# A delta-rule recurrence feeding a cosine-gated network: block inverses in halves for the first two pairs, and the cosine's argument in radians

## The chip, the cores and the metric

The kernel runs on one core of a Trainium2 chip. The metric is the device time of one execution in microseconds; the time before is 710.78 us, the median of three runs (709.21 to 710.8). The profile shown below is of one execution of 709.21 us; from its first to its last instruction it spans 707.4 us, and all times of the profile count from its start.

The engines have these names: PE is TensorE (matmul; PEld its weight loads), DVE is VectorE, ACT is ScalarE, POOL is GpSimd, SP is SyncE, which here only issues DMA transfers. All five run side by side and wait for one another by semaphores. Each takes its own instructions in order.

## The reference

Two stages. The first is a delta rule for 4 × 8 heads, 768 steps, head dimension 48; the second is a network with the gate h · cos(h).

```python
# q, k, v: (4, 8, 768, 48), beta: (4, 8, 768); all float32
k_n = k / (norm(k, axis=-1) + 1e-6)
state = zeros((B, H, D, D))
for t in range(S):
    y[:, :, t] = einsum('bhd,bhde->bhe', q[:, :, t], state)
    v_old = einsum('bhde,bhd->bhe', state, k_n[:, :, t])
    state = state + bt[..., None, None] * einsum('bhd,bhe->bhde', k_n[:, :, t], v[:, :, t] - v_old)

x = y.transpose(0, 2, 1, 3).reshape(3072, 384)
h = x @ w_in            # 384 x 2048
g = h * cos(h)
out = g @ w_out         # 2048 x 384
```

## The kernel before

**Units and pairs.** The 768 steps are cut into 24 units of C = 32 steps; two units make a pair, so there are 12 pairs. Within a unit the 32 steps depend on each other through a strictly lower triangular 32 × 32 matrix L per head (the products of keys, scaled by beta): the new values u solve (1 + L) u = r, with r the values less what the state holds for the keys. The kernel computes Z = (1 + L)⁻¹, which needs no state and so can be made ahead, and applies it by matmuls when the state arrives.

**The inverse.** For a pair, the matrices of 2 units × 8 heads × 4 batches stand one per partition (64, each twice: the two halves of the partitions take every other row of Z). The tile gb comes there through DRAM, since the rearrangement goes across partitions. The elimination takes one column j at a time, two operations each. Pair 0 is done on VectorE with Z in PSUM, all others on GpSimd with Z in SBUF. Z then goes through DRAM again (z_dr) and comes back as zt, arranged for TensorE.

```python
def invert(m, tag, columns):
    a, z = gbs[m], zs[m]
    eng = nc.gpsimd if tag is None else nc.vector
    for j in columns:                       # 31 of them
        rows = j // SPLIT + 1
        shape = [128, rows, C - 1 - j]
        ...
        eng.tensor_tensor(out=part, in0=z[:, 0:rows, j, None].to_broadcast(shape),
                          in1=a[:, j, None, j + 1 :].to_broadcast(shape), op=ALU.mult)
        behind = z[:, 0:rows, j + 1 :]
        eng.tensor_tensor(out=behind, in0=behind, in1=part, op=ALU.subtract)
```

**A unit's way through the recurrence.** turn (transposes of k and q) and gram (products of keys, and of keys and queries) prepare a unit. Then come, in a chain from unit to unit:

```python
through_state(n)   # PE:  p_kq <- st, kq_t          keys and queries times the state
right_side(n)      # DVE: rhs = vp - p_kq           (unit 0: rhs is vp)
solve(n)           # PE:  p_u <- zt, rhs            32 small matmuls
solve_out(n)       # DVE: u = p_u * bz
update(n)          # PE:  p_s <- kp, u
update_out(n)      # DVE: st = st + p_s
within(n)          # PE:  p_kq += tt, u
within_out(n)      # ACT: y <- p_kq
features(n)        # PE:  p_z <- transposes of y
features_out(n)    # ACT: x_ffn <- p_z              half of the pair's 256 tokens
```

p_u and p_z use the same PSUM bank ("one"), of which there is a single buffer.

**The network.** For a pair (256 tokens), eight blocks of two hidden tiles pass through:

```python
def hidden(p, f):          # PE: p_h <- x_ffn, w_in; 6 float32 matmuls, 12 records in the trace; two PSUM buffers
TURN = 1.0 / (2.0 * math.pi * SCALE)

def hidden_turns(p, f):    # ACT: whole turns, as int32
    nc.scalar.activation(turns[p, f], p_hs[p, f], AF.Copy, scale=TURN)

def hidden_rest(p, f):     # DVE, one operation: the rest, in turns
    nc.vector.scalar_tensor_tensor(out=r, in0=p_hs[p, f], scalar=TURN, in1=turns.pop((p, f)),
                                   op0=ALU.mult, op1=ALU.subtract)

def hidden_cos(p, f):      # ACT, two operations
    nc.scalar.activation(r, r, AF.Abs)
    nc.scalar.activation(r, r, AF.Sin, bias=halfpi, scale=-2.0 * math.pi)

def hidden_gate(p, f):     # DVE: g_ffn = r * p_h; frees the buffer of p_h
```

The products with w_out follow: plain for pair 0, and for all other pairs by Strassen's scheme (7 products for 8, with sums of parts of g_ffn and of w_out made on VectorE). The weights arrive as float64 words and are narrowed in the kernel: 12 tiles of w_in and 16 of w_out, each with two operations on ScalarE, two on VectorE and one on GpSimd.

**The order.** The kernel adds each of these steps as a task with an engine, an assumed cost, what it depends on, which buffers it takes and by when it is due. A list scheduler in Python (`Order`) then lays the tasks out in the order in which they are emitted and pins each engine's instructions to that order. So a change of assumed costs or dues moves instructions everywhere. [...] A few of its settings:

```python
WINDOW = 133.06; STICK = 4.14
W_IN, W_OUT, LOADS = 62.2, 48.42, -16.83
START = 64.59; FIRST, STEP = 4.18, 5.64      # dues of the blocks of the network
```

Of the kernel before, what the change touches and what calls it, by code (L numbers as in the profile page):

```python
# [11 lines left out]
FP = mybir.dt.float32  # L12
# [5 lines left out]
C = 32  # L18
DP = 64
SPLIT = 2  # L20


SCALE = 256.0


def _consts():

    p = np.arange(128)
    share = p // 64
    row = SPLIT * np.arange(C // SPLIT)[None, :] + share[:, None]
    return np.concatenate(
        [
            np.eye(128),
            p[:, None] % C < np.arange(C)[None, :],
            p[:, None] // C % 2 == np.arange(2)[None, :],  # L40
            (row[:, :, None] == np.arange(C)).reshape(128, -1),
        ],
        axis=1,
    ).astype(np.float32)


class Order:
# [8 lines left out]

    WINDOW = 133.06
    LAG = {"PE": 0.2, "DVE": 0.15, "ACT": 0.15, "POOL": 0.2, "SP": 2.0}
    IN_FLIGHT = 8
    STICK = 4.14  # L60
    CHANGE = 0.15
    SMALL = ("gram", "state", "solve", "update", "within")


    BLOCK, PHASE, AHEAD, FETCH = 256, 63, 38, 3.5
    COUNT = {
        "turn": 16, "gram": 128, "state": 256, "solve": 128, "update": 64, "within": 128,
        "features": 6, "hidden": 24, "out": 16,
# [151 lines left out]
def kernel(  # L220
# [43 lines left out]
    ROWS = C // SPLIT  # L264
    GBS, ZS = 2, 2
    GATES = 9
    LEAD = 3
# [65 lines left out]
    consts = const.tile(list(consts_np.shape), FP, name="consts")  # L333
    near = 130 + C
    for cols in (slice(0, near), slice(near, consts_np.shape[1])):
# [3 lines left out]
    odd = consts[:, 128 + C : 130 + C]  # L339
    eye = consts[:, 130 + C :].rearrange("p (r i) -> p r i", i=C)  # L340

# [173 lines left out]
    def gram_keys(n):  # L515
        g = gs[n] = work.tile([128, H, C], FP, name="g")
        bs = scales[n // 2][0][:, n % 2]
        nc.vector.tensor_tensor(
            out=by_parity(g),
            in0=p_gs[n][:, :, :, 0],  # L520
            in1=bs.rearrange("p (j a) -> p a j", a=2)[:, :, :, None].to_broadcast(wide),
            op=ALU.mult,
        )
# [10 lines left out]
    def gram_put(n):  # L534
        m = n // 2
        if m not in gbs:
            gbs[m] = dram.tile([2, H, B, C, C], FP, name="g_dr")
        nc.sync.dma_start(
            out=gbs[m][n % 2].rearrange("h b j i -> (b j) h i"), in_=gs.pop(n)
        )  # L540
# [11 lines left out]
    def invert_eye(m, tag):  # L552
# [4 lines left out]
        nc.scalar.copy(zs[m], eye)  # L557

    def invert(m, tag, columns):

        a, z = gbs[m], zs[m]
        eng = nc.gpsimd if tag is None else nc.vector
        for j in columns:
            rows = j // SPLIT + 1
            shape = [128, rows, C - 1 - j]
            if tag is None:
                part = work.tile([128, ROWS * C // 2], FP, name="part")  # L570
            else:
                part = ffn_pool.tile([128, ROWS * C // 2], FP, name="part_v", tag="o")
            part = part[:, 0 : shape[1] * shape[2]].rearrange(
                "p (r i) -> p r i", i=shape[2]
            )
            eng.tensor_tensor(  # L576
                out=part,
                in0=z[:, 0:rows, j, None].to_broadcast(shape),
                in1=a[:, j, None, j + 1 :].to_broadcast(shape),
                op=ALU.mult,  # L580
            )
            behind = z[:, 0:rows, j + 1 :]
            eng.tensor_tensor(out=behind, in0=behind, in1=part, op=ALU.subtract)  # L583
# [55 lines left out]

    def solve(n):  # L640
        zt, rhs = zts.pop(n), rhss.pop(n)
        p_u = p_us[n] = bank("one", [128, H, D], "p_u")
        for h in range(H):
            for b in range(B):
                nc.tensor.matmul(  # L645
                    p_u[quarter(b), h], zt[quarter(b), h], rhs[quarter(b), h]
                )

    def solve_out(n):

        u = us[n] = work.tile([128, H, 2, D], FP, name="u")
        wide = [128, H, 2, D]
        nc.vector.tensor_tensor(  # L653
            out=u,
            in0=p_us.pop(n)[:, :, None, :].to_broadcast(wide),
            in1=scales[n // 2][1][:, n % 2, :, :, None].to_broadcast(wide),
            op=ALU.mult,
        )
# [68 lines left out]

    TURN = 1.0 / (2.0 * math.pi * SCALE)

    def hidden_turns(p, f):  # L730
        turns[p, f] = ffn_pool.tile([128, 2, TOK], I32, name="turns")
        nc.scalar.activation(turns[p, f], p_hs[p, f], AF.Copy, scale=TURN)  # L732

    def hidden_rest(p, f):
        r = rests[p, f] = ffn_pool.tile([128, 2, TOK], FP, name="r")
        nc.vector.scalar_tensor_tensor(  # L736
            out=r, in0=p_hs[p, f], scalar=TURN, in1=turns.pop((p, f)),
            op0=ALU.mult, op1=ALU.subtract,
        )

    def hidden_cos(p, f):
        r = rests[p, f]
        nc.scalar.activation(r, r, AF.Abs)  # L743
        nc.scalar.activation(r, r, AF.Sin, bias=halfpi, scale=-2.0 * math.pi)  # L744

# [116 lines left out]
    def store(p, i):  # L862
# [9 lines left out]
            two=1, kq=1, one=1, h=2, vp=2, ksum=2, scales=4, kq_t=LEAD + 1,  # L872
            tt=LEAD + 1, g_gram=2, g_dr=3, gb=GBS, z=ZS, z_dr=3, zt=2, rhs=2, u=2, y=2,
            x=2, turns=2, r=2, g=GATES, o=2, o_out=2,
# [4 lines left out]
    VECTOR = {0: "one"}  # L879
    W_IN, W_OUT, LOADS = 62.2, 48.42, -16.83  # L880
    PLAIN = range(1)
    outs_done = [None]
    START = 64.59
    FIRST, STEP = 4.18, 5.64
    BASE = [START + (8 * FIRST + (p - 1) * 8 * STEP if p else 0) for p in range(NU // 2 + 2)]

    def inverse(m):
# [8 lines left out]
        deps = [("eye", m), ("gram_get", m)]  # L896
        ends = [0, 4, 8, 12, 16, 20, 24, C - 1]
        for i, (x, y) in enumerate(zip(ends, ends[1:])):
            each = (0.2, 0.001) if held else (0.323, 0.00178)
            cost = sum(  # L900
                2 * (each[0] + each[1] * (j // SPLIT + 1) * (C - 1 - j)) for j in range(x, y)
            )
            add(("inv", m, i), "DVE" if held else "POOL", cost,
                lambda x=x, y=y: invert(m, held, range(x, y)), deps,
                uses=[("gb", m)] if y == C - 1 else [])
            deps = [("inv", m, i)]
# [7 lines left out]
    def unit(n):  # L914
# [55 lines left out]
        if second:  # L970
# [9 lines left out]
            uses=[("vp", m)] if n else [])  # L980
        add(("solve", n), "PE", 0.75, lambda: solve(n), [("right", n), ("get", n)],
            makes=[("one", ("p_u", n))], uses=[("zt", n), ("rhs", n) if n else ("vp", m)])
        add(("solve_out", n), "DVE", 1.0, lambda: solve_out(n), [("solve", n), scaled],
# [17 lines left out]
    def gated(p):  # L1001
        for f in range(0, FT, 2):
# [3 lines left out]
            if p or f:  # L1006
# [6 lines left out]
                [("hidden", *key)], makes=[("turns", ("turns", *key))])  # L1013
            add(("rest", *key), "DVE", 0.73, lambda f=f: hidden_rest(p, f),
                [("turns", *key)], makes=[("r", ("r", *key))], uses=[("turns", *key)])
# [170 lines left out]
```

## Time and profile before

| what | value |
|---|---|
| time, median of 3 | 710.78 us |
| span of the profile | 707.4 us |
| PE busy | 642.0 us, 91% |
| DVE busy | 400.3 us, 57% |
| POOL busy | 344.1 us, 49% |
| ACT busy | 281.5 us, 40% |
| granted TensorE clock, mean | 0.955 |

The page of a profile gives, for each engine, its busy time, then the span in 40 equal slices with the busy share of each in tenths (9 is 90% or more), and the granted clock of TensorE in tenths of full speed. A group of instructions is named by its line in the kernel, its engine and "output<-inputs"; x is how often it ran, and the idle time of its engine ahead of it is given with what ended it. A busy TensorE is not one at its peak: the ends of matmuls are modelled. In the timeline a row is: start in us, duration in us, engine, line, operation, and in brackets the idle time ahead of it with what ended that.

### The profile page before, as it was taken

What the parts mean: (1) busy time and instruction counts of PE and PEld (TensorE: products, weight loads), DVE (VectorE), ACT (ScalarE), POOL (GpSimd) and SP (SyncE); (2) the same over time, 40 slices, a digit from 0 to 9 for tenths busy, and PEclk for the clock granted to TensorE, in tenths of its full rate; (3) what the DMA queues carried; (4) which work ended last, traced back from release to release, by engine and by line L of the source; (5) the groups of instructions that cost most, each with busy time, mean ns of one, the idle gap of its engine ahead of it and who ended that gap; (6) DMA issues with size and microseconds to landing.
All of it is one profiled execution on the core that took longest, in us unless ns stands there. A gap on an engine that the chain in (4) does not pass through costs nothing.

```text
span 707.4 us, 25090 instructions
## 1 busy us (share of the span) xinstructions
PE 642.0 (91%) x11000; PEld 564.3 (80%) x11000; DVE 400.3 (57%) x804; ACT 281.5 (40%) x482; POOL 344.1 (49%) x738
## 2 busy tenths in 40 slices
PE   3206989999999999999999999999999999999985
PEld 2205767768988988988988988988989989988975
DVE  4995568967655645546546546545635535544441
ACT  4423467742443532532533533533433433432420
POOL 6468957868608508518518518518318328200000
PEclk9555899999999999999999999999999999999999
DMA  9888663562223233133223133231221220100000
GB/s 176 211 161 197 122 193 80 135 125 58 36 56 71 39 64 67 32 74 66 45 60 66 29 77 64 38 74 37 38 51 37 37 52 14 31 23 4 1 23 22
DMA packets 162700, 49.25 MB, mean 70 GB/s; under 512 B 154208, under 2 KB 157296, under 8 KB 162592
## 3 DMA queue, kind: packets, MB, share of 16 engines
q1 hardware_dynamic: 161120, 46.82, 32.1%
q8 instruction: 86, 1.41, 0.9%
q0 software_dynamic: 384, 0.64, 0.4%
q10 hardware_dynamic: 1088, 0.20, 0.2%
q14 instruction: 22, 0.18, 0.1%
HBM read 36.62 MB, written 11.01 MB: 67 GB/s over the span
## 4 chain that ended last, share of the span: by engine, by line
PE 85%; DMA 4%; POOL 3%; DVE 3%; issue 2%; ACT 1%; SPq 1%; ACTq 0%; DVEq 0%; POOLq 0%
PE p_h L719 35%; PE p_out L805 30%; PE p_kq L618 4%; PE p_kq L683 3%; PE p_s L666 3%; PE p_out L761 3%; PE p_u L645 3%; PE p_t L489 2%; PE p_g L507 2%; DMA pairs<-in_moe_w_in_dram 2%; POOL part L576 1%; POOL z L583 1%; DMA qp<-in_q_dram 1%; DMA gb<-g_dr 1%; DMA kp<-in_k_dram 1%
## 5 line engine op out<-in xcount | busy, mean ns | idle before, releaser
L719 PE MATMUL p_h<-x_ffn,w_in 128*128 128x256 f32 x1152 | 264.9, 383 | 2.4 <-DVE g_ffn L751 1.6
L719 PEld LDWEIGHTS p_h<-x_ffn,w_in 128*128 128x128 f32 x1152 | 216.9, 191 | 32.0 <-DVE g_ffn L751 1.5
L576 POOL TENSOR_TENSOR part<-z,gb 128x126 f32<-128x126 f32 (+22 forms) x341 | 136.1, 399 | 210.7 <-DMA gb<-g_dr 185.3
L583 POOL TENSOR_TENSOR z<-z,part 128x126 f32<-128x126 f32 (+22 forms) x341 | 134.3, 394 | 26.7
L805 PE MATMUL p_out<-w_out,g_ffn 128*128 128x192 f32 x704 | 133.6, 334 | 2.8 <-DVE o L853 1.6
L736 DVE SCALAR_TENSOR_TENSOR r<-p_h,turns 128x512 f32<-128x512 f32 x96 | 66.1, 689 | 113.8 <-ACT turns L732 113.7
L732 ACT ACTIVATE turns<-p_h 128x512 int32<-128x512 f32 x96 | 56.9, 592 | 169.1 <-PE p_h L719 169.0
L805 PEld LDWEIGHTS p_out<-w_out,g_ffn 128*128 128x128 f32 x704 | 113.6, 190 | 9.5 <-ACT o L842 3.3
L805 PE MATMUL p_out<-w_sum,g_ffn 128*128 128x192 f32 x528 | 96.3, 329 | 1.8 <-DVE o L853 1.8
L751 DVE TENSOR_TENSOR g_ffn<-r,p_h 128x512 f32<-128x512 f32 x96 | 65.6, 683 | 48.0 <-ACT r L744 48.0
L805 PEld LDWEIGHTS p_out<-w_sum,g_ffn 128*128 128x128 f32 x528 | 86.3, 190 | 4.9 <-DVE o L853 3.1
L821 DVE TENSOR_TENSOR g_ffn<-g_ffn 128x256 f32<-128x256 f32 x176 | 80.5, 480 | 10.8 <-PE p_out L805 8.9
L743 ACT ACTIVATE r<-r 128x512 f32<-128x512 f32 x96 | 60.7, 632 | 58.2 <-DVE r L736 58.1
L744 ACT ACTIVATE r<-r,halfpi 128x512 f32<-128x512 f32 x96 | 69.3, 722 | 3.1
L853 DVE SCALAR_TENSOR_TENSOR o<-p_out,o 128x192 f32<-128x192 f32 x77 | 26.5, 356 | 59.7 <-PE p_out L805 59.2
L489 PE MATMUL p_t<-consts,kp 128*128 128x128 f32 x96 | 16.9, 306 | 41.9 <-DMA vp<-in_v_dram 29.5
L489 PEld LDWEIGHTS p_t<-consts,kp 128*128 128x128 f32 x96 | 12.9, 157 | 44.6 <-issue 38.5
L694 ACT COPY y<-p_kq 128x384 f32<-128x384 f32 x24 | 11.5, 478 | 76.7 <-PE p_kq L683 76.7
L448 POOL TENSOR_TENSOR knrm<-ksum,halves 128x16 f32<-128x16 f32 (+1 forms) x14 | 36.4, 2602 | 9.8 <-DVE ksum L436 7.6
L618 PEld LDWEIGHTS p_kq<-st,kq_t 48*32 48x32 f32 x2944 | 29.5, 106 | 9.6 <-issue 8.8
L618 PE MATMUL p_kq<-st,kq_t 48*32 48x48 f32 x2944 | 33.1, 215 | 3.9 <-issue 3.2
L653 DVE TENSOR_TENSOR u<-p_u,bz 128x768 f32<-128x768 f32 x24 | 23.0, 956 | 17.1 <-PE p_u L645 17.1
(65 smaller groups left out, 547.0 us busy)
## 6 DMA issues: line engine op xcount, KB each, us to landing
pairs<-in_moe_w_in_dram SPq DMA_DIRECT2D x12, 512.0 KB
gb<-g_dr SPq DMA_DIRECT2D x24, 256.0 KB
pairs<-in_moe_w_out_dram SPq DMA_DIRECT2D x16, 384.0 KB
vp<-in_v_dram SPq DMA_DIRECT2D x96, 48.0 KB
out_dram<-o SPq DMA_DIRECT2D x24, 192.0 KB
kp<-in_k_dram SPq DMA_DIRECT2D x92, 48.0 KB
qp<-in_q_dram SPq DMA_DIRECT2D x92, 48.0 KB
g_dr<-g SPq DMA_DIRECT2D x24, 128.0 KB
```

Source lines behind the costliest of these rows:

```text
L489: nc.tensor.transpose(p_t[:, a, j], src[:, 2 * j : 2 * j + 2], ident)
L576: eng.tensor_tensor(out=part, in0=z[:, 0:rows, j, None].to_broadcast(shape), in1=a[:, j, None, j + 1 :].to_broadcast(shape), op=ALU.mult,)
L583: eng.tensor_tensor(out=behind, in0=behind, in1=part, op=ALU.subtract)
L618: nc.tensor.matmul(p_kq[quarter(b), par, a, j], kq_t[rows48(par), a, j, quarter(b)], st[rows48(par), b // 2, j, b % 2], start=(j == 0 and ...
L719: nc.tensor.matmul(p_h[:, i], w_in[:, t, (f + i) * 128 : (f + i + 1) * 128], xts[p][:, t], start=(t == 0), stop=(t == KT - 1),)
L732: nc.scalar.activation(turns[p, f], p_hs[p, f], AF.Copy, scale=TURN)
L736: nc.vector.scalar_tensor_tensor(out=r, in0=p_hs[p, f], scalar=TURN, in1=turns.pop((p, f)), op0=ALU.mult, op1=ALU.subtract,)
L743: nc.scalar.activation(r, r, AF.Abs)
L744: nc.scalar.activation(r, r, AF.Sin, bias=halfpi, scale=-2.0 * math.pi)
L751: nc.vector.tensor_tensor(out=gates[p, f // 4][:, f % 4 : f % 4 + 2], in0=rests.pop((p, f)), in1=p_hs.pop((p, f)), op=ALU.mult,)
L805: nc.tensor.matmul(p_o, left(p, e // 2, a)[:, e % 2], right(e, b), start=(e == 0), stop=(e == FT // 2 - 1), skip_group_check=True,)
L821: nc.vector.tensor_tensor(out=left(p, k, to), in0=left(p, k, one), in1=left(p, k, two), op=op)
```

## The change

It has two parts, which replace one another in the sense that the kernel after has the first and not the second.

**Halves.** For pairs 0 and 1 only the two diagonal 16 × 16 blocks of 1 + L are inverted, both in the same operations (one more dimension of two). Z is then the inverse of the block diagonal part alone, and what lies below it is handled in the solve, with vectors: v = Z r gives the first 16 rows of u; a cross product with L of the first half, subtracted from the second half of r; and a second product with Z. For this the tile g of a unit is kept in SBUF until its cross product. The aim is a shorter inverse at the start, where everything waits for the first one. The tile u has one buffer instead of two.

**Radians.** The cosine's argument is no longer kept in turns. The rest is h less 2π times the whole turns, and 2π stands in two parts for accuracy, so hidden_rest has two VectorE operations per block where it had one. The scheduler's cost for it is set to 1.45 instead of 0.73, and its settings are other ones.

```diff
-    WINDOW = 133.06
-    STICK = 4.14
+    WINDOW = 82.51
+    STICK = 2.55
...
+    HALVED = range(2)
+    GRAMS = 4
...
     def invert(m, tag, columns):
...
+        n = C // 2 if m in HALVED else C
         for j in columns:
             rows = j // SPLIT + 1
-            shape = [128, rows, C - 1 - j]
+            shape = [128, rows, n - 1 - j]
+            if n < C:
+                shape = [128, 2] + shape[1:]
...
+                column = twice(column, (ROWS // 2) * C + n)
+                row = twice(row, n * C + n)
+                behind = twice(behind, (ROWS // 2) * C + n)
...
+    def solve_half(n):
+        p_us[n] = bank("one", [128, H, D], "p_u")
+        quarters(p_us[n], zts[n], rhss[n])
+
+    def half_out(n):
+        v = us[n] = work.tile([128, H, D], FP, name="y")
+        nc.scalar.activation(v, p_us.pop(n), AF.Copy, scale=first_half)
+
+    def cross(n):
+        p_us[n] = bank("one", [128, H, D], "p_u")
+        quarters(p_us[n], gs.pop(n), us.pop(n))
+
+    def cross_out(n):
+        rhs = work.tile([128, H, D], FP, name="rhs")
+        nc.vector.scalar_tensor_tensor(
+            out=rhs, in0=p_us.pop(n), scalar=less_second, in1=rhss[n],
+            op0=ALU.mult, op1=ALU.add,
+        )
+        rhss[n] = rhs
...
     def hidden_rest(p, f):
         r = rests[p, f] = ffn_pool.tile([128, 2, TOK], FP, name="r")
+        n = turns.pop((p, f))
         nc.vector.scalar_tensor_tensor(
-            out=r, in0=p_hs[p, f], scalar=TURN, in1=turns.pop((p, f)),
-            op0=ALU.mult, op1=ALU.subtract,
+            out=r, in0=n, scalar=-PI2_HI * SCALE, in1=p_hs[p, f], op0=ALU.mult, op1=ALU.add
+        )
+        nc.vector.scalar_tensor_tensor(
+            out=r, in0=n, scalar=-PI2_LO * SCALE, in1=r, op0=ALU.mult, op1=ALU.add
         )
...
-    W_IN, W_OUT, LOADS = 62.2, 48.42, -16.83
+    W_IN, W_OUT, LOADS = 57.87, 99.73, 3.15
-    START = 64.59
-    FIRST, STEP = 4.18, 5.64
+    START = 35.79
+    FIRST, STEP = 3.55, 5.99
...
+        if m in HALVED:
+            ends = [0, 4, 8, C // 2 - 1]
...
-            add(("rest", *key), "DVE", 0.73, lambda f=f: hidden_rest(p, f),
+            add(("rest", *key), "DVE", 1.45, lambda f=f: hidden_rest(p, f),
                 [("turns", *key)], makes=[("r", ("r", *key))], uses=[("turns", *key)])
```

In the order of the changed kernel, the first blocks of p_h again stand right behind the chain of unit 1, and each of units 0 to 3 has its half-solve, cross product and solve in a row, with other work of TensorE between some of them.

## The prediction

> **What bounds the kernel now.** I read the page's slices first, then the busy time by stage, then the timeline of the first 80 us, then the waits of TensorE after it. The slices (40 of 17.7 us; digits are tenths):
>
> ```profile
> PE   3206989999999999999999999999999999999985
> DVE  4995568967655645546546546545635535544441
> PEclk9555899999999999999999999999999999999999
> DMA  9888663562223233133223133231221220100000
> ```
>
> TensorE is full from about the fifth slice to the end. Before that it is mostly idle at half clock while the DMA engines are full. The first matmul of the network (p_h, L719) stands at 79.15 us, so I cut the span there, at 160 and at 675:
>
> ```profile
> 0.00:79.15 79.15, 30.60 (x950) 25.81 (x951) 54.59 (x147) 29.48 (x53) 52.68 (x90) 0.63 0.86 178
> 79.15:160.00 80.85, 76.13 (x1109) 59.13 (x1103) 59.47 (x108) 49.42 (x91) 61.36 (x95) 0.98 0.56 132
> 160.00:675.00 515.00, 512.46 (x8823) 458.90 (x8822) 277.39 (x526) 200.29 (x335) 230.11 (x556) 1.00 0.24 46
> ```
>
> (Columns: busy us and count of PE, PEld, DVE, ACT, POOL; clock; DMA share; GB/s.) In the long middle TensorE idles 2.5 of 515 us: nothing but less TensorE work can shorten it. In the second stretch it idles 4.7 us. Only the head has room: 48.5 idle us. The two longest waits of TensorE after the head hardly count:
>
> ```profile
> PE p_h L719 <- issue: 0.8, 2, 0.6
> PE p_out L805 <- DVE o L853: 0.4, 2, 0.2
> ```
>
> So the span is the time of the first p_h plus a nearly fixed 628 us of TensorE work. What fixes 79.15 is in the timeline:
>
> ```profile
> 27.63 0.19 DVE L576 TENSOR_TENSOR part_v<-p_i,gb 128x31 f32<-128x31 f32 x1 [0.50 <-DMA gb<-g_dr]
> 45.57 0.18 DVE L583 TENSOR_TENSOR p_i<-p_i,part_v 128x16 f32<-128x16 f32 x1
> 46.79 0.69 SPq L592 DMA_DIRECT2D z_dr<-z  x1
> 52.42 4.53 SPq L601 DMA_DIRECT2D zt<-z_dr  x8
> 57.04 2.01 PE L645 MATMUL p_u<-vp,zt 32*32 32x48 f32 x64 [1.65 <-issue]
> 79.15 5.45 PE L719 MATMUL p_h<-x_ffn,w_in 128*128 128x256 f32 x24
> ```
>
> The first inverse runs on VectorE from 27.63 to 45.75. It is stored to DRAM at 46.79 and fetched back by eight issues from 52.42 to 56.95. The first solve starts at 57.04, and the recurrence through units 0 and 1 takes 22.1 us more. SyncE issues almost without a pause from 0.75 to 70 us (a load of four DMAs takes it 1.9 to 4.3 us). That queue is as much a limit of the head as the inverse is.
>
> **What the Trainium skill says.** "VectorE: DVE Perf Modes", section on the errata: an fp32 operation with two tensors takes (N+151)/0.96 ns, so 691 ns for 512 elements. The trace agrees: 689 ns for r<-p_h,turns. The same page, section "Why `tensor_tensor` can't do 2×_2P or 4×", says the second tensor occupies the second read port. So I give the new second operation no faster mode, although it reads SBUF only; the SBUF-only L410 of this shape has a median of 686 ns. "TensorE: Matmul & The Clock Gate", Part 1: the clock is halved until TensorE has been busy for a few microseconds. The trace agrees: clock 0.63 in the head, and a solve of 64 matmul records takes 1.55 to 2.01 us there and 0.88 us at 88.5 us. "DMA: Bandwidth & Descriptors", section on small descriptors, says short ones cost more per byte; 154,208 of the 162,700 packets here are under 512 B, in agreement with DMA at 0.86 and only 178 GB/s in the head.
>
> **The change, part by part.**
>
> *Inverse of pair 0.* It had 31 columns of two operations and has now 15, of 16 to 72 elements. In the trace a column of 30 elements takes 0.48 us from start to start, 56 to 58 take 0.52, 81 take 0.56. My sum over the 15 new shapes is 7.5 us against 18.15 measured. VectorE ends it at about 35.2: **10.6 us earlier**.
>
> *What arrives of that at the solve.* The instruction order shows SyncE's queue unchanged up to the weight load issued at 39.13; the store of z follows at once, at about 39.6 (it was 46.79). Then come the loads of the next k, q and v and one weight load, which took 39.57 to 46.68 in the trace, and then the fetch of zt, from about 47.2 instead of 52.42. So **5.2 of the 10.6 us arrive**, and the first half-solve starts at about 51.8.
>
> *Added to the chain of each unit of pairs 0 and 1.* One solve becomes solve, masked copy on ScalarE, cross product, subtraction on VectorE, solve. At the head's clock I take 1.55 us for each added set of matmuls, 0.48 for the copy (as L694, same shape), 0.56 for the subtraction (as L633), and some 0.6 for four hand-overs. That is 4.7 us; 9.4 for two units, less some 0.8 where the turn of unit 5 now fills a gap between two steps: 8.6. One link I checked apart: by the order, unit 0's subtraction also stands behind the scale of pair 2, whose power on GpSimd comes after the second inverse, near 53, then 1.3 us on VectorE. It meets the cross product at about 56 and should cost little. The old chain has 4.8 us of idle TensorE in its 22.1 us (waits of 0.6 to 1.2 us for u, tt, x and y); I let 1.4 of them be filled by work that now falls there. **First p_h: 79.15 − 5.2 + 8.6 − 1.4 = 81.15, that is +2.**
>
> *Inverse of pair 1 on GpSimd.* 30 instead of 62 operations; it started at 38.86 and ended at 73.7. Mine ends near 50 (15 columns of 0.7 us, and a few slowed ones). This frees GpSimd for the weight additions 20 us earlier. But these did not gate the first p_h: the first three weight tiles were added by 26.3. So I give it no gain beyond the second stretch.
>
> *Units 2 and 3.* They pass when TensorE is already full: two added sets of 0.88 us each, 3.5 us of new TensorE work. **+3.5.**
>
> *Radians in place of turns.* All 96 blocks get a second VectorE operation of 0.69 us: 66 us of new work. In the middle some 80 of them fall: 277 + 55 = 332 of 515 us, 65% busy. A block's way from p_h back to a free buffer is lengthened by 0.69; there are two buffers. In the trace two blocks run back to back at 279.10 and 286.88: block B's gate ends at 288.92, its buffer is asked for at 289.47, only 0.55 us of slack. The new order, though, mostly puts single blocks between products, so I expect small waits: **+1.0** over the whole middle. In the second stretch 15 operations add 10.3 us and two subtractions 1.1: 59.5 + 11.4 = 70.9 of 80.85, 88% busy, in order, with dependent steps. **+2.5.** The tail ends in products and collects as before: 0.
>
> *Recovered.* Of the 4.7 idle us of the second stretch I let 1.5 vanish.
>
> Sum: 710.8 + 2.0 + 3.5 + 1.0 + 2.5 − 1.5 = 718.3, so **718 us**.
>
> **Rivals.** *(a) The head really shortens.* If the old chain's 22.1 us are mostly waits that the new steps fill, the first p_h comes at about 74 and the total at 711 or below. For it: TensorE idles 48.5 us in the head. Against: these waits are on the chain's own predecessors and on weights that still arrive at the pace of a full DMA. I know of no route to a gain beyond 2% (under 696.6): the first p_h would have to stand near 60. *(b) VectorE becomes the bound of the middle.* If the extra 0.69 us hits each p_h that comes back to its buffer, 80 blocks times 0.1 to 0.2 us make 8 to 16 us, and the total is 726 to 734. For it: the slack of 0.55. Against: 65% busy, and an order laid for the longer operation. *(c) DMA takes the gain and more.* The store and fetch of z move into the slices where DMA is at 0.8 to 0.9; if they land 3 to 5 us late, the first p_h is at 85 and the total near 722.
>
> **Range and chances.** The first p_h may err by 5 us, the second stretch by 4, the middle by 6; together some 9 us, more room upwards: 708 to 731. The upper limit of "within 2%" is 725.0; I give slower by over 2% one chance in five, the rest to within.
>
> **What would show it.** In the profile after: the inverse on VectorE in 30 operations from about 27.6 to 35; the store of z at 39 to 40, the fetch at 47; the first solve at 51 to 53; the first p_h at 79 to 84; two r operations a block of 0.69 us; VectorE at about 88% between the first p_h and 160, near 65% in the middle; TensorE idle there at most 5 us. A first p_h below 76 would make my chain too long; over 10 us of TensorE waits on g_ffn or r in the middle would be rival (b).

## The result, and the profile after

The kernel after takes 720.9 us (median of four runs, 719.4 to 721.68), the kernel before in the same comparison 710.79 us: a ratio of 1.0145, 95% interval 1.0122 to 1.0168. The kernel after is slower by about 10 us, or 1.5%. The profiled executions span 717.6 and 707.4 us, which is the difference to be explained: 10.2 us.

The page of the kernel after, the same slices as shown of before:

```profile
PE   3217799899999999999999999999999999999985
DVE  4825589896765676666667666666666556664641
PEclk9655899999999999999999999999999999999999
DMA  9876582562223043043053052142042220100000
```

VectorE is lighter in the second and third slice (8 and 2, where it had 9 and 9: the halved inverse) and heavier in the long middle (mostly 6, where it had 5). TensorE fills later: its fifth slice reads 7, where it read 9.

The busy time by stage, cut at the first half-solve (54.31), the first p_h (85.38), then 166.23 and 685; columns as before:

```profile
0.00:54.31 54.31, 13.90 (x296) 11.03 (x297) 28.10 (x89) 19.88 (x36) 32.40 (x55) 0.73 0.86 179
54.31:85.38 31.07, 21.39 (x910) 18.23 (x911) 15.89 (x26) 11.01 (x21) 9.97 (x8) 0.65 0.59 131
85.38:166.23 80.85, 77.39 (x1353) 60.33 (x1346) 70.80 (x121) 48.53 (x90) 55.82 (x96) 0.98 0.57 134
166.23:685.00 518.77, 513.53 (x8834) 459.51 (x8833) 334.86 (x612) 203.80 (x339) 243.07 (x550) 1.00 0.24 46
```

The first p_h is at 85.38 us and was at 79.15: 6.2 of the 10.2 us are lost in the head. From there to the end it is 632.2 us, and was 628.2: the other 4.0. After the head TensorE is as full as it was.

The timeline of the head of after, answering to the one of before (start, duration, engine, line, output<-input; in brackets the idle time ahead and what ended it):

```profile
28.25 0.19 DVE L606 TENSOR_TENSOR part_v<-p_i,gb 128x30 f32<-128x30 f32 x1 [0.93 <-DMA gb<-g_dr]
35.46 0.18 DVE L607 TENSOR_TENSOR p_i<-p_i,part_v 128x16 f32<-128x16 f32 x1
39.56 0.39 SPq L616 DMA_DIRECT2D z_dr<-z  x1
40.00 4.72 SPq L333 DMA_DIRECT2D kp<-in_k_dram  x4
49.74 4.28 SPq L625 DMA_DIRECT2D zt<-z_dr  x8
54.31 1.89 PE L669 MATMUL p_u<-vp,zt 32*32 32x48 f32 x64 [13.30 <-DMA zt<-z_dr]
56.88 1.50 PE L669 MATMUL p_u<-y,g 32*32 32x48 f32 x64 [0.67 <-ACT y L679]
58.89 0.61 DVE L687 SCALAR_TENSOR_TENSOR rhs<-p_u,consts,vp 128x384 f32<-128x384 f32 x1
59.56 1.50 PE L669 MATMUL p_u<-rhs,zt 32*32 32x48 f32 x64 [1.18 <-DVE rhs L687]
```

The inverse ends at 35.64 instead of 45.75, 10.1 us earlier. The store is issued at 39.56, 7.2 us earlier; the fetch at 49.74, 2.7 us earlier; and the first solve starts 2.7 us earlier. Three quarters of the gain are gone before TensorE sees any of it. Part of the loss is a cost that the store brings with it: the load that SyncE issues directly behind the store is slow, whichever it is. In the kernel before it was the load of v, here it is the load of k. In e5 below, where ScalarE issues the store, the same load of k is fast. Before, and then e5:

```profile
47.53 4.30 SPq L323 DMA_DIRECT2D vp<-in_v_dram  x4
```

```profile
43.11 1.91 SPq L333 DMA_DIRECT2D kp<-in_k_dram  x4
```

Of the 4.72 us in after, the first of the four issues takes 3.24 and the others 0.44 to 0.45. In all ten profiles in which SyncE issues this store, the issue behind it takes 2.8 to 3.2 us. The store itself has landed at 44.98, in the kernel before at 52.03; so in after the fetch stands 4.8 us in SyncE's queue when its data are already there, in before 0.4. What then follows can be cut at four marks (start of unit 0's first solve, its u, unit 1's first solve, its u, first p_h):

| stretch | before | after | difference |
|---|---|---|---|
| unit 0: first solve to u | 2.05 | 6.82 | +4.77 |
| u to unit 1's first solve | 8.50 | 9.61 | +1.11 |
| unit 1: first solve to u | 2.07 | 8.12 | +6.05 |
| u to first p_h | 9.49 | 6.52 | −2.97 |
| sum | 22.11 | 31.07 | +8.96 |

8.96 less the 2.73 that the first solve starts earlier makes the 6.2 us.

The chain that ended last, in the head of after (start, duration, what):

```profile
49.25 4.45 DMA pairs<-in_moe_w_in_dram
53.72 0.68 ACT w_in L416
54.40 0.56 ACT pairs L418
54.98 1.53 DVE pairs L422
56.52 0.34 DVE w_in L427
56.97 1.29 DVE krec L473
58.89 0.62 DVE rhs L687
59.56 1.55 PE p_u L669 x64
```

The inverse is not on it. The solve of unit 0 is released by the subtraction (rhs, L687), which stands on VectorE behind the narrowing of a weight tile and the scale of pair 2 (krec); and that tile's load was issued at 49.25, behind the loads of k, q and v. So two chains arrive within half a microsecond of each other: zt, half-solve and cross product, whose last matmul ends at about 58.4, and the weight tile with the scale, which ends at 58.9.

### The profile page after: what moved, and what is told of

Its sections match the earlier page's. It is cut to its first block, busy times and chain, and to the rows that moved or that the text cites. A ratio compares the mean times of both kernels' runs of the same rounds, so it can differ in the third digit from the quotient of the medians.

```text
span 717.6 us, 26144 instructions
## 1 busy us (share of the span) xinstructions
PE 649.1 (90%) x11512; PEld 569.6 (79%) x11512; DVE 459.2 (64%) x872; ACT 285.5 (40%) x486; POOL 341.3 (48%) x706
## 4 chain that ended last, share of the span: by engine, by line
PE 83%; DVE 5%; DMA 4%; issue 3%; ACT 2%; SPq 2%; POOL 0%; ACTq 0%; DVEq 0%
PE p_h L768 34%; PE p_out L858 29%; PE p_kq L642 4%; PE p_u L669 3%; PE p_kq L732 3%; PE p_s L715 3%; PE p_out L814 3%; PE p_t L501 2%; PE p_g L519 2%; DMA qp<-in_q_dram 2%; SPq L333 2%; DMA pairs<-in_moe_w_in_dram 1%; PE p_z L749 1%; DVE pairs L422 1%; DVE o L906 1%
## 5 line engine op out<-in xcount | busy, mean ns | idle before, releaser
L606 POOL TENSOR_TENSOR part<-z,gb 128x30 f32<-128x30 f32 (+24 forms) x325 | 133.4, 410 | 125.3 <-DMA gb<-g_dr 100.9
L607 POOL TENSOR_TENSOR z<-z,part 128x30 f32<-128x30 f32 (+24 forms) x325 | 133.5, 411 | 25.5
L858 PE MATMUL p_out<-w_out,g_ffn 128*128 128x192 f32 x704 | 130.8, 333 | 3.5 <-DVE o L906 1.6
L787 DVE SCALAR_TENSOR_TENSOR r<-turns,p_h 128x512 f32<-128x512 int32 x96 | 65.8, 685 | 80.5 <-ACT turns L780 80.3
L796 ACT ACTIVATE r<-r 128x512 f32<-128x512 f32 x96 | 60.4, 629 | 107.7 <-DVE r L790 106.4
L790 DVE SCALAR_TENSOR_TENSOR r<-turns,r 128x512 f32<-128x512 int32 x96 | 69.6, 725 | 3.3
L797 ACT ACTIVATE r<-r,halfpi 128x512 f32<-128x512 f32 x96 | 69.3, 722 | 3.1
L501 PE MATMUL p_t<-consts,kp 128*128 128x128 f32 x96 | 17.4, 310 | 24.3 <-DVE tt L539 13.5
L507 ACT COPY kq_t<-p_t 128x512 f32<-128x512 f32 x48 | 25.7, 588 | 14.8 <-PE p_t L501 14.8
```

The lines of the kernel that those rows point to most:

```text
L606: eng.tensor_tensor(out=part, in0=column, in1=row, op=ALU.mult)
L787: nc.vector.scalar_tensor_tensor(out=r, in0=n, scalar=-PI2_HI * SCALE, in1=p_hs[p, f], op0=ALU.mult, op1=ALU.add)
L790: nc.vector.scalar_tensor_tensor(out=r, in0=n, scalar=-PI2_LO * SCALE, in1=r, op0=ALU.mult, op1=ALU.add)
L797: nc.scalar.activation(r, r, AF.Sin, bias=halfpi, scale=-1.0 / SCALE)
L858: nc.tensor.matmul(p_o, left(p, e // 2, a)[:, e % 2], right(e, b), start=(e == 0), stop=(e == FT // 2 - 1), skip_group_check=True,)
```

## The experiments

The accounts that the expectations set against each other: *latency* (the added steps stand on the chain of the head, and the second VectorE operation of the radians is mostly beside it), *VectorE* (the radians make VectorE the limit), *settings* (the scheduler's other numbers made the difference), and for the head *queue* (SyncE's in-order queue keeps the fetch of zt back). One table for all runs: "work" is TensorE's busy time in the profile, "idle" the span less that (so a slower clock shows up as work), "rest" the span from the first p_h on.

| kernel | median us | ratio to before (95%) | us over before by the ratio | span | work | idle | first p_h | rest |
|---|---|---|---|---|---|---|---|---|
| before | 710.8 | 1 | 0 | 707.4 | 642.0 | 65.4 | 79.2 | 628.2 |
| after | 720.9 | 1.0145 (1.0122 to 1.0168) | +10.3 | 717.6 | 649.1 | 68.5 | 85.4 | 632.2 |
| e1_turns | 718.2 | 1.0092 (1.0059 to 1.0124) | +6.5 | 715.6 | 648.8 | 66.8 | 85.4 | 630.2 |
| e2_radians | 723.9 | 1.0169 (1.0134 to 1.0203) | +12.0 | 722.1 | 649.0 | 73.1 | 79.0 | 643.1 |
| e3_halves | 722.1 | 1.0142 (1.011 to 1.0173) | +10.1 | 721.0 | 650.8 | 70.2 | 86.3 | 634.7 |
| e4_nohalf | 724.2 | 1.0166 (1.0125 to 1.0207) | +11.8 | 724.1 | 645.3 | 78.8 | 78.7 | 645.4 |
| e5_actz | 723.6 | 1.015 (1.0115 to 1.0185) | +10.7 | 722.3 | 653.0 | 69.3 | 89.8 | 632.5 |
| e6_hold | 721.2 | 1.0118 (1.0097 to 1.0139) | +8.4 | 719.8 | 652.3 | 67.5 | 86.8 | 633.0 |
| e7_both | 718.4 | 1.009 (1.0062 to 1.0118) | +6.4 | 716.5 | 652.7 | 63.8 | 83.6 | 632.9 |
| e8_nocross | 716.6 | 1.0052 (1.0035 to 1.0069) | +3.7 | 714.2 | 644.5 | 69.7 | 77.8 | 636.4 |
| e9_half1 | 730.8 | 1.0286 (1.0259 to 1.0314) | +20.3 | 728.4 | 648.7 | 79.7 | 85.3 | 643.1 |
| e10_relaid | 718.8 | 1.012 (1.0088 to 1.0153) | +8.5 | 715.8 | 643.7 | 72.1 | 78.7 | 637.1 |
| e11_before_head | 711.1 | 1.0006 (0.9992 to 1.0019) | +0.4 | 712.7 | 644.1 | 68.6 | 81.4 | 631.3 |
| e12_turns_both | 717.4 | 1.0086 (1.0059 to 1.0113) | +6.1 | 715.6 | 651.3 | 64.3 | 85.8 | 629.8 |

The runs were made on different occasions, and the medians of before in their own comparisons lie between 710.8 and 712.4. So totals are compared by the ratios; the column beside them is the ratio's excess times 710.8 us, good to about 2 us. Span, work, idle, first p_h and rest are of one profiled execution each.

### The two parts, one at a time

**e1_turns:** the kernel after with the one operation of turns, everything else and the order kept.

```diff
-        n = turns.pop((p, f))
-        nc.vector.scalar_tensor_tensor(
-            out=r, in0=n, scalar=-PI2_HI * SCALE, in1=p_hs[p, f], op0=ALU.mult, op1=ALU.add
-        )
-        nc.vector.scalar_tensor_tensor(
-            out=r, in0=n, scalar=-PI2_LO * SCALE, in1=r, op0=ALU.mult, op1=ALU.add
-        )
+        nc.vector.scalar_tensor_tensor(
+            out=r, in0=p_hs[p, f], scalar=TURN, in1=turns.pop((p, f)),
+            op0=ALU.mult, op1=ALU.subtract,
+        )
...
-        nc.scalar.activation(r, r, AF.Sin, bias=halfpi, scale=-1.0 / SCALE)
+        nc.scalar.activation(r, r, AF.Sin, bias=halfpi, scale=-2.0 * math.pi)
```

> The kernel after with the one VectorE operation in turns, its assumed cost left at 1.45, so that every instruction keeps its place and only 96 operations of 0.72 us are gone. Latency theory (the loss is the longer chain of units 0 and 1, plus the matmuls of units 2 and 3): 718 to 720.5 us, first p_h still near 85. VectorE theory (the 70 us of added VectorE work are the loss): 711 to 713, with the gain spread over the whole span.

718.2 us, the latency account's figure and not the VectorE account's. That is +6.5 us over before, where after has +10.3. The first p_h does not move (85.4), the rest goes from 632.2 to 630.2. In this order 96 operations of 725 ns (0.69 us predicted), 69.6 us of VectorE, cost 3.8 us by the ratios and 2.0 in the profiled spans: say 2 to 4.

**e2_radians:** the kernel before with the two operations, its order kept (the reverse of the edit above).

> The kernel before with the two VectorE operations in radians, the assumed cost left at 0.73, so that every instruction keeps its place. Latency theory: 712 to 714.5 us, the first p_h at 79 as before, small waits of p_h on the gate in the middle because this order leaves only 0.55 us of slack. VectorE theory: 718 to 721.

+12.0 us, at 723.9: above both accounts, the latency account's figure missed by some 10 us and the VectorE account's by 3. The first p_h is where it was; all of the loss, 15 us of the profile's span, lies in the rest. The waits of TensorE after the first p_h:

```profile
PE p_h L723 <- DVE g_ffn L758: 6.6, 11, 3.1
PE p_kq L622 <- issue: 4.5, 3, 3.5
```

In the kernel before, p_h waited 1.6 us for g_ffn in this stretch. That is 5 us more, not 15; the table puts about half of the loss under "work", although the matmuls are the same. The timeline shows how a wait comes to cost more than its length. The same block of p_h, in the kernel before and then in this one:

```profile
137.83 2.86 PE L719 MATMUL p_h<-x_ffn,w_in 128*128 128x256 f32 x12 [1.28 <-DVE g_ffn L751]
```

```profile
142.55 5.49 PE L723 MATMUL p_h<-x_ffn,w_in 128*128 128x256 f32 x12 [3.15 <-DVE g_ffn L758]
```

The wait is 1.9 us longer, and the twelve matmuls behind it take 5.49 instead of 2.86 us: 4.5 us lost by a buffer that came back 1.9 us late. By the block after the next, 8.0 of the 15 us are lost (it starts at 155.82, before at 147.86); the other 7 go little by little until the end and were not itemized. The Trainium skill, "TensorE: Matmul & The Clock Gate", Part 1, says that the clock falls to half after an idle window of about 3.4 us and comes back after as much work; the 1.28 us wait without a penalty agrees, while the 3.15 us wait had one below that figure. The mean granted clock from the first p_h to 160 us fell from 0.98 to 0.92.

**e10_relaid:** e2 with the scheduler told of it, so that the order is laid again for the longer VectorE work.

```diff
-            add(("rest", *key), "DVE", 0.73, lambda f=f: hidden_rest(p, f),
+            add(("rest", *key), "DVE", 1.45, lambda f=f: hidden_rest(p, f),
```

> The kernel before with radians, and the scheduler told so (cost 1.45 instead of 0.73 for the two operations): the order is laid again for the longer VectorE work, with the kernel before's other settings. With the old order radians took 723.9 us. If the loss of 12 us came from an order laid for one operation, this kernel takes 713 to 717 us, with less than 3 us of waits of p_h on g_ffn. If it comes from the second operation itself, in whatever order, it takes 721 to 725 us as before.

+8.5 us, at 718.8, between the two figures. Of e2's 12.0 us, 3.5 go by the ratios (6.3 by the spans) when the order is laid for two operations: TensorE's work is again within 1.7 us of before, and p_h waits 0.3 us for g_ffn, once. But 718.8 is above the 713 to 717 us that an order laid for it was to give. The longest sum there is now p_out waiting for the collecting VectorE operations (o, L860): 9.9 us in 13 waits, 3.4 in 8 in the kernel before. So radians cost 2 to 4 us in the order of after, about 8 in this one, and 12 in an order laid for turns.

**e3_halves:** halves and turns with the kernel before's settings of the scheduler.

```diff
-    WINDOW = 82.51
+    WINDOW = 133.06
-    STICK = 2.55
+    STICK = 4.14
-    W_IN, W_OUT, LOADS = 57.87, 99.73, 3.15
+    W_IN, W_OUT, LOADS = 62.2, 48.42, -16.83
-    START = 35.79
-    FIRST, STEP = 3.55, 5.99
+    START = 64.59
+    FIRST, STEP = 4.18, 5.64
...
-            add(("rest", *key), "DVE", 1.45, lambda f=f: hidden_rest(p, f),
+            add(("rest", *key), "DVE", 0.73, lambda f=f: hidden_rest(p, f),
```

The edit of e1 is in it too.

> Halves alone: the kernel before with the halved inverses of two pairs, turns kept, and the scheduler's settings of the kernel before. Latency theory: 716 to 721 us with the first p_h at 84 to 88. VectorE theory: 710 to 712. Settings theory (the loss is what the other settings of the scheduler do to the order): 709 to 712 as well, and then the next run slow.

+10.1 us, at 722.1, a little above the latency account's 716 to 721 and far from the 709 to 712 of the two others: the halves alone cost that with the settings of before, with the first p_h at 86.3. With the settings of after (e1) they cost 6.5, so the other settings are not what makes the kernel after slower; the two intervals overlap a little, and whether they help is not settled. Nor does any run give the tile u its second buffer back; in the profile of after, the operation that writes u waits for p_u only (8 times, 6.3 us), so the one buffer does not hold it up directly.

**e4_nohalf:** the kernel after with `HALVED = range(0)`: whole inverses and one solve, radians, the settings of after.

> The kernel after with no pair halved (radians and the settings of the kernel after stay). Latency theory: 711 to 715 us, first p_h at 77 to 80. VectorE theory and settings theory: 717 to 721.

+11.8 us, at 724.2, above the 711 to 715 of the one account and the 717 to 721 of the others. The head is short again (78.7), but the rest takes 645.4 us. The loss comes early: from the first p_h to the 25th block of the network it is 164.3 us (before 147.5, after 153.8), and from there to the end 481.1 (480.7 and 478.4). Radians without halves cost 12 us, here and in e2; halves without radians 6.5 to 10; both together 10.3. The parts do not add. A reading that fits, not tested by itself: a kernel that gets to its first p_h later has more of its weights and of its VectorE work behind it there, and waits less for them in the second stretch.

**e9_half1:** `HALVED = range(1)`: pair 1 with its whole inverse on GpSimd.

> The changed kernel with halves for pair 0 only: pair 1 (units 2 and 3) keeps its whole inverse on GpSimd and its single solve. The prediction's own sum puts 3.5 us of TensorE work on the halves of pair 1. If that term holds, this kernel takes 716.5 to 718.5 us, with the first block of the network at 85 to 86.5 as in the changed kernel, and the gain lies between the first block and block 24. Rival: in the second stretch VectorE is 88% busy and TensorE waits for it, so the order counts for more than the 3.5 us of matmuls; then this kernel is between 720 and 724.

+20.3 us, 10 us slower than after, where the prediction's term of 3.5 us for units 2 and 3 would have made it faster; 730.8 is also well above the rival's 720 to 724. TensorE has nearly the same work and 11 us more idle time. The longest wait is at 156.5, for g_ffn, 6.6 us:

```profile
PE p_h L768 <- DVE g_ffn L804: 10.3, 5, 6.6
```

The chain in front of it:

```profile
148.70 1.33 POOL w_out L431
150.05 3.24 DMA pairs<-in_moe_w_out_dram
153.31 0.54 ACT w_out L416
153.85 0.43 ACT pairs L418
154.28 0.53 ACT r L796
154.84 0.73 ACT r L797
155.66 0.70 DVE g_ffn L804
156.49 4.40 PE p_h L768 x12
```

The cosine (r, L796) stands on ScalarE behind the narrowing of a weight tile, whose load could only start when GpSimd had released a buffer. It is the pattern of the head: an operation that TensorE needs stands in order behind one that waits for a weight. GpSimd ends the second inverse at 70.3 us here and at 50.6 in the kernel after. That this delay is the cause of the late tile at 150 us was not tried; the order differs in many places.

### Where the head's gain goes

**e8_nocross:** the kernel after without half-solve, mask, cross product and subtraction. This leaves the lower left quarter of the matrices of pairs 0 and 1 out of the computation, so it shows what the added steps cost and is no version to be used.

```diff
-        if m in HALVED:
+        if False:
             add(("solve_half", n), ...)
```

> The kernel after without the half-solve, the masked copy, the cross product and the subtraction: only the shorter inverses are left, and the lower left quarter of each matrix of pairs 0 and 1 is left out of the computation. Latency theory: first p_h at 76 to 79, and 708 to 712 us: the added steps cost some 9 to 12 us, and the shorter inverse alone would have brought 2 to 3 over the kernel before with radians' cost of 3 in it. VectorE theory: 716 or more.

```profile
53.47 1.83 PE L669 MATMUL p_u<-vp,zt 32*32 32x48 f32 x64 [13.15 <-DMA zt<-z_dr]
77.77 7.29 PE L768 MATMUL p_h<-x_ffn,w_in 128*128 128x256 f32 x24
```

Without the added steps the first p_h comes 7.6 us earlier (85.4 to 77.8). The total falls by 6.6 us by the ratios (3.4 by the spans), to 716.6 and not to the 708 to 712 that the latency account gave: in the profile the rest grows from 632.2 to 636.4. Even with nothing added to the solve, a shorter inverse brings the first p_h from 79.15 to 77.8, that is 1.4 of the 10 us. The first solve starts 3.6 us earlier than before; the chain from there takes 24.3 us where it took 22.1, with 4.4 us in three stops of TensorE that nothing in the profile ends (0.7 in one before). The scheduler has laid the order again here, so the 7.6 us are the added steps together with what the order does.

**e5_actz:** store and fetch of pair 0's inverse (for unit 0) issued by ScalarE, past SyncE's queue.

```diff
     def put(m):
+        eng = nc.scalar if m == 0 else nc.sync
...
-        nc.sync.dma_start(
+        eng.dma_start(
...
-            nc.sync.dma_start(out=zts[n][quarter(b)], in_=z_dr[b])
+            (nc.scalar if n == 0 else nc.sync).dma_start(out=zts[n][quarter(b)], in_=z_dr[b])
```

> The kernel after, with the store of pair 0's inverse and the fetch of unit 0's zt issued by ScalarE instead of SyncE; nothing else moves. Two-limits theory (unit 0 is held twice, by SyncE's queue in front of zt, and by weight tile 7, which stands on ScalarE ahead of the masked copy and on VectorE ahead of the subtraction): the first half-solve at about 49 instead of 54.3, but the subtraction still at 56 to 58, so 717.5 to 720.5 us. Queue theory (SyncE's queue alone holds the head): first p_h 5 us earlier, 715 to 716.

+10.7 us, at 723.6, above both figures and no better than after: the half-solve starts at 49.6, 4.7 us earlier, and the first p_h comes 4.4 us later. Between them:

```profile
47.28 0.66 ACT L416 ACTIVATE w_in<-pairs 128x512 f32<-128x512 f32 x1 [4.15 <-DMA pairs<-in_moe_w_in_dram]
47.34 1.04 ACTq L626 DMA_DIRECT2D zt<-z_dr  x2
51.67 1.74 PE L670 MATMUL p_u<-vp,zt 32*32 32x48 f32 x60 [0.31 <-DMA zt<-z_dr]
58.03 0.66 ACT L416 ACTIVATE w_in<-pairs 128x512 f32<-128x512 f32 x1 [7.60 <-DMA pairs<-in_moe_w_in_dram]
59.13 0.57 ACT L680 ACTIVATE y<-p_u,consts 128x384 f32<-128x384 f32 x1
59.75 1.50 PE L670 MATMUL p_u<-y,g 32*32 32x48 f32 x64 [6.34 <-ACT y L680]
```

The masked copy waits on ScalarE behind the narrowing of a weight tile that lands at 58. The queue account falls as the sole cause: the weight tile is a second limit. But the edit does not take the first limit away cleanly. The store lands at 42.25, and its fetch, now on ScalarE, stands behind the narrowing of an earlier weight tile until 47.34, 5.1 us more. And SyncE, which the profile shows waiting 2.0 us for the store, issues the load of the later weight tile at 53.14 instead of 49.25; the tile lands 4.3 us later than in after, and the last solve of unit 0 starts 3.4 us later. So e5 shows that the first half-solve alone does not set the first p_h, and not what the queue alone costs.

**e6_hold:** only the second limit removed. The narrowing of weight tiles 7 to 10, the scale of pair 2 and the weighing of pair 1 are emitted behind named steps of units 0 and 1 (a table in the scheduler: if a task of the table comes up early, it is held until the named one is out).

```diff
+HOLD = {("split", 7): ("half_out", 0), ("shift", 7): ("solve_out", 0), ("add", 7): ("solve_out", 0),
+        ("scale", 2, 0): ("solve_out", 0), ...}
...
-                emit()
+                if key in HOLD and HOLD[key] not in emitted:
+                    held.setdefault(HOLD[key], []).append((key, emit))
```

> The kernel after, with the narrowing of weight tiles 7 to 10, the scale of pair 2 and the weighing of pair 1 moved behind the steps of units 0 and 1 that they stood ahead of on ScalarE and VectorE; zt still from SyncE. Two-limits theory: the half-solve stays at 54, the subtraction at 58.5 instead of 58.9, so 719 to 721 us. Weights theory (the weight tiles alone hold the head): 714 to 716.

+8.4 us; the interval overlaps with that of after, and the first p_h is at 86.8. Now the subtraction follows the cross product at once:

```profile
57.65 1.50 PE L681 MATMUL p_u<-y,g 32*32 32x48 f32 x64 [0.67 <-ACT y L691]
59.22 0.62 DVE L699 SCALAR_TENSOR_TENSOR rhs<-p_u,consts,vp 128x384 f32<-128x384 f32 x1 [10.06 <-PE p_u L681]
```

VectorE had idled 10 us ahead of it, and it starts no earlier: zt is the limit here.

**e7_both:** both edits.

> Both edits of the two runs before together. Two-limits theory: the half-solve at 49, the subtraction at 53, the first p_h at 77 to 80, and 712 to 716 us, more than the two gains together. If the chain of matmuls itself is the bound of the head, 718 or more.

+6.4 us, at 718.4, 3.9 less than after, with intervals that do not overlap, but above the 712 to 716 of the two-limits account. The solve of unit 0 starts at 53.7, 5.9 us earlier than in after; alone, neither edit moved it forward (62.99 and 59.89, after 59.56). But the first p_h is only 1.8 us earlier, and the chain shows where the rest went:

```profile
61.29 1.70 PE p_kq L655 x110
63.15 3.42 issue
66.57 1.15 PE p_g L531 x55
69.24 2.97 DMA kp<-in_k_dram
```

3.42 us in which TensorE's sequencer waits for nothing that the profile shows, and then the turn of a later unit waits for its keys. Each limit that is taken away uncovers another within a few us. Here too the fetch stands behind a weight tile on ScalarE, until 45.39, when the store has landed at 40.33.

**e12_turns_both:** e7 with turns (the edit of e1). It looks for the best version with halves.

> The changed kernel with turns instead of radians, with both head edits (store and fetch by ScalarE; narrowing of weight tiles and scale held back). If the parts add up (radians cost 2.7 us, the two head edits together 2.5), this takes 715 to 717 us. If what comes after the first block swallows one of them, as it swallowed 3 of the 7.6 us when the added steps were left out, it takes 717.5 to 719 us. Either way it stays above the kernel before.

+6.1 us, at 717.4; the interval overlaps with those of e1 and e7, so no gain of turns and head edits together over either alone is shown. The first p_h is at 85.8, 2.2 us later than in e7. It stays above the kernel before.

**e11_before_head:** the kernel before with the edit of e5, and weight tile 7 and the scale of pair 2 held behind unit 0's solve as in e6.

> The kernel before, with whole inverses and turns, but with the store of pair 0's inverse and its fetch for unit 0 issued by ScalarE, and the narrowing of weight tile 7 and the scale of pair 2 behind unit 0's solve. If the queue of SyncE costs the kernel before what the trace suggests (store 1.0 us after the inverse, fetch 5.6 us after the store), the solve of unit 0 starts at 52 to 54 instead of 57, the first block comes at 74 to 77, and the kernel takes 706 to 709 us. Rival: SyncE's other loads become the limit instead, as in the changed kernel with the same edit; then the first block comes at 78 to 81 and the time is 710 to 714 us.

711.1 us, the same as before (1.0006, 0.9992 to 1.0019), first p_h 81.4: about the rival's figures, for another reason. ScalarE in this run:

```profile
46.67 0.40 ACTq L605 DMA_DIRECT2D z_dr<-z  x1
53.52 1.87 ACTq L614 DMA_DIRECT2D zt<-z_dr  x4
```

With nothing on ScalarE between the two, the fetch is issued 6.85 us after the store; it was 5.63 in the kernel before, through SyncE's full queue. What the fetch depends on is the store, 256 KB that must land while the DMA engines are nearly full. It lands 5.2 us after its issue in the kernel before, 6.8 here, 5.4 in after and 4.4 in e5 and e7, and the fetch cannot come sooner, whatever the queue.

No version with halves came below the kernel before. None of them fetched as soon as the store had landed, which in after, e5 and e7 would be 4.8 to 5.1 us earlier; what that is worth was not run.

## Why the prediction was right, and where it was not

718 us was predicted for the kernel after, 708 to 731 as the range, and the most likely outcome within 2%: 720.9 us and +1.5% lie there. By its steps:

- **Inverse of pair 0**: right. 30 operations from 28.25 to 35.64, 7.4 us (predicted 7.5, end at 35.2). The store at 39.56 (39.6) as well, and the inverse of pair 1 on GpSimd, which ends at 50.6 (near 50).
- **What arrives at the solve**: mis-sized. "5.2 of the 10.6 us arrive", with the fetch at 47.2 and the first half-solve at 51.8; it was 49.74 and 54.31, and 2.7 us arrive. The step took the SyncE loads behind the store with the durations that they had before, when they did not stand behind it: the load of k took 4.72 us instead of 1.92, in e6 and e8 4.7 as well. That is the cost of the place behind the store, 2.8 us here, and the kernel before shows it too, in the 4.30 us of the load of v. Why the issue behind the store is slow was not tried.
- **The added chain**: the step per unit was right for unit 0 (+4.77 us, predicted 4.7). Unit 1 was mis-sized: +6.05 where 4.7 less 0.8 was given; the chain shows a stop of 1.98 us at 76.56 inside its last solve, released by nothing in the profile (the last section returns to it), and the turn of unit 5 between solve and cross product. What is filled was underrated as well: 2.97 us after unit 1's u, less 1.1 before its solve, where 1.4 was given. Sum +8.96, predicted 7.2. e8, without the added steps, has its first p_h 7.6 us earlier.
- **The link "checked apart"** (subtraction behind the scale of pair 2): right in time, a cost of half a microsecond. But it is a second limit at almost the same place, which e5 and e6 show: neither it nor the fetch can be moved alone with profit. The prediction did not see that.
- **First p_h +2.0**: it was +6.2, at 85.4, outside the 79 to 84 that the prediction named as its sign. Rival (c) had the first p_h at 85 and the total near 722, and is the closest description, though its reason is not quite what happened: the fetch was issued 2.5 us later than forecast, while its way from issue to solve took 4.6 us as before, and the longer chain did the rest.
- **After the head** the prediction had +3.5 (units 2 and 3), +1.0 and +2.5 (radians), −1.5 recovered: +5.5. It was +4.0. e1 divides it: without radians the rest is 2.0 us above before (predicted 3.5 − 1.5 = 2.0), and radians bring 2.0 us in the spans and 3.8 by the ratios (predicted 3.5). VectorE's second stretch is 70.80 of 80.85 us (predicted 70.9), the middle 334.86 of 518.77, 65%, and TensorE idles 5.2 us there. Rival (b) did not come true in this order. In the order of before more of it does: e2 is 12.0 us over before.
- **Units 2 and 3, +3.5**: right as matmul time (four sets of 64 at 0.88 us), wrong as a separable cost. e9 takes these sets away and is 10 us slower.

So the total was near because two errors had opposite signs: 4.2 us too little in the head, 1.5 too much after it. That part is luck, and the range was wide enough to hold rival (c)'s 722 as well. The mechanism, the gain of the inverse used up by the transfer and by the longer solve, is shown by the marks of the timeline and supported by e8; how the rest of the loss divides between halves, radians and the order is known only to some 2 us.

## What to carry to other kernels

A shorter step on a chain is worth only what reaches the next consumer: here 10.1 us at the inverse were 7.2 at the store's issue and 2.7 at the fetch, because a DRAM round trip and an in-order queue lie between, and even with nothing added to the solve the first p_h gained only 1.4 (e8). When a transfer moves to another place in a queue, what it costs its follower moves with it. And a transfer put on another engine to escape a queue stands in that engine's queue. Before moving one thing, look for what arrives second: two edits that alone did not bring the solve forward brought it forward by 5.9 us together. And when an operation on an in-order engine gets longer, lay the order again: the same second operation cost 2 to 4, 8 or 12 us, depending on the order.

## What the runs showed of the hardware that was not expected

- A wait of TensorE can have a second price: 1.28 us (before) cost 1.28, 3.15 us (e2) cost 3.15 and 2.6 more in slower matmuls. Its length alone does not decide: in after, a wait of 1.73 us at 136.90 had slow matmuls behind it (4.51 us for twelve), in e4 one of 2.08 us at 100.75 had none.
- TensorE stops of 1.98 us (after), 3.42 (e7) and 3.48 (e2) in the middle of a group of small matmuls, with no releaser in the profile ("issue"). They are not scattered. Count the matmuls and weight loads of the trace from 0: behind the start of the first solve, every such stop of 0.25 us or more, in all 14 profiles, stands at place 193 or 194 of a block of 256 (those three at 1985, 1474 and 2754). And the pages list a DMA queue of the kind "instruction" with one packet per 256 of these records (22,145 before, 23,172 after); packets, MB and share, before and after:

```profile
q8 instruction: 86, 1.41, 0.9%
q8 instruction: 90, 1.47, 0.8%
```

  So TensorE seems to wait there for its next 256 instructions. That is inferred from the counts, and no run was made to test it; the scheduler of both kernels reckons with it (BLOCK = 256).
- The clock column of the head cannot be relied on. Before, and then e10_relaid, from 60 to 70 us (the column after the brackets' last is the clock):

```profile
60.00:70.00 10.00, 8.02 (x355) 7.01 (x355) 5.45 (x13) 3.99 (x8) 9.00 (x15) 0.50 0.93 205
```

```profile
60.00:70.00 10.00, 8.33 (x355) 6.86 (x351) 6.09 (x13) 4.55 (x8) 8.90 (x17) 1.00 0.94 203
```

The clock reads 0.50 and 1.00, the 355 matmuls take 8.02 and 8.33 us. The first solve's matmuls have medians of 276 and 277 ns in the two, against 201 ns for the shape at full speed. The Trainium skill says in the same part, under the caveats on the trace, that such events are unreliable on trn2; these runs agree, and the duration of a known matmul is the better clock.
